# Reordering the front of a three-stage kernel: loads, order of work, constant matmuls, and the step of the sums

## The chip, the cores and the metric

The kernel runs on one core of a Trainium2 chip. The metric is device time in microseconds (us) of one execution; the median over several runs is compared. The engines are TensorE (PE, matmuls and transposes), VectorE (DVE), ScalarE (ACT), GpSimd (POOL) and SyncE (SP, which here issues nearly all DMAs).

## The reference, cut to what matters

```
# attention with 32 memory slots a head; B=4, H=8, S=576, D=64, M=32
a      = softmax(phi, over S)                     # S x M
k_m    = a.T @ k ;  v_m = a.T @ v                 # M x D each
attn   = softmax(q @ k_m.T / 8, over M)
x      = attn @ v_m                               # 2304 tokens x 512
# a gated layer, d_ff = 1536
x      = (sigmoid(x @ w_gate) * (x @ w_val)) @ w_out
# a router over 8 experts (noisy, top 2), each: relu(x @ w1[e]) @ w2[e], F = 1024
out    = sum over the two experts of weight * expert(x)
```

## The kernel before, in words

All of it is one launch. Matrix products in 16-bit floats are made of a high and a low half of each operand, so that one product takes three matmuls. The weights of the gated layer come as 64-bit words. A job is one block of 256 columns of `w_gate` or `w_val` (`wg`, `wv`, six each) or 256 rows of `w_out` (`wo`, six); each job has two half blocks of 512 KB. `rounded` (lines 371 to 381) turns a half block into floats: ScalarE converts the low words (375), VectorE does two operations on the high words (379, 380), GpSimd adds (381). After both half blocks ScalarE sums their squares (404), and `norm2` (86) makes from these a power of two as scale: a matmul with ones and some small VectorE operations.

The value memory of a batch is multiplied into the weights (`fold`, 245 to 266): `vs` is made on GpSimd (252), 32 small matmuls (259) give the folded weights of one unit `u` of 256 columns, ScalarE casts the high half (261) and VectorE makes the low half (263; for the first fold line 1102). Stage 1 (`stage1`, 476) multiplies the folded weights with the attention weights `x` of 192 tokens (line 488, 24 matmuls of 192 columns), then gates: ScalarE 490, VectorE 492, ScalarE 493, VectorE 494. Stage 2 (line 505) multiplies with `wo`. Then come tokens, router and the experts.

The attention of a batch (`attend`, 1053) is a generator: `features` (two groups of four heads: maximum 229, exponential 231), `memory` for each group (transposes of phi 189 and 194, their copies 192 and 195, the contraction with keys and values 204, its copy 206, transposes 212, copies 216 and 218), then `attention`: `scores` for the two groups' first 512 tokens and for the 64 left over (matmuls 284 and 281, maximum 288, subtraction 292, exponential 293), `normalised` (sum 299, then 303 or 305, reciprocal 306, multiplication on GpSimd 307), and `turned` (transposes 315, high half 324, low half 325). `values_scale` (237) gives the scale of the values.

The order on each engine follows priority. Attention runs ahead of the rest by 1000 in the front. `behind(d, o)` orders one instruction after another on an engine without a semaphore. `turns(g, ...)` advances generators by one step. `build` starts with `att_first_loads(0)`, whose order is SP's issue order; then three steps of attention, `FIRST` = 5 steps of weights, and attention on until the first scores. From there `half()` advances the weights by one half block and one step of attention follows, until the tokens of batch 0 are ready; the first `fold` is issued as soon as its scales exist. The VectorE steps of `scores`, `normalised` and `turned` are ordered behind the last half block (`self.shifted`). Then stage 1 runs over six units of batch 0, with weights and the attention of batch 1 between. PSUM pools: `pg` of 4 banks, `px` and `pr` of 2 each.

## Time and profile before

| | before |
|---|---|
| median of 3 runs | 849.76 us (848.55 to 851.15) |
| profiled execution | 845.65 us, span 843.8 us |
| TensorE busy | 799.6 us (95%) |
| VectorE busy | 455.0 us (54%) |
| ScalarE busy | 440.5 us (52%) |
| GpSimd busy | 233.3 us (28%) |

The span is the time from the first to the last recorded instruction of the profiled execution. Busy shares are means over stages with different limits, so what bounds a stage is read from that stage alone. A row of a timeline merges neighbouring instructions of one line; its time is that from the start of the first to the end of the last. Matmuls overlap, so the time of a run divided by its count gives their pace, and the mean duration of one does not.

### The profile page before, as it was taken

To read this page: it belongs to the slowest core of one execution; us is meant where nothing else is said; L and a number is where in the kernel's file an instruction comes from. 1 tells how busy PE (TensorE), PEld (TensorE's weight loads), DVE (VectorE), ACT (ScalarE), POOL (GpSimd) and SP (SyncE) were. 2 spreads that over 40 slices of the span, in tenths; PEclk is the share of its full clock that TensorE was granted. 3 is DMA by queue.
4 is the path that set the end of the run, shared out by engine and by line. 5 is a ranking of instruction groups with operands and counts; after the bars stand their busy time and mean duration, and the time that the engine had idled before them with its cause. 6 is when DMAs were issued, how large, how long until landed. Compare 5 with 4: busy or idle time off the path is not lost.

```text
span 843.8 us, 16766 instructions
## 1 busy us (share of the span) xinstructions
PE 799.6 (95%) x6555; PEld 528.5 (63%) x6555; DVE 455.0 (54%) x1223; ACT 440.5 (52%) x860; POOL 233.3 (28%) x258
## 2 busy tenths in 40 slices
PE   5699789999999999999999999999999999999995
PEld 3478656576677766776566565746657475574753
DVE  3788987363748698655472365543445344450210
ACT  4677786154545576534163476645556364461321
POOL 1755640012203040231135442023133231322012
PEclk9999989999999999999999999999999999999998
DMA  9987758421132656617948899536767757473103
GB/s 310 367 250 241 236 186 291 131 82 27 31 93 59 204 171 177 228 40 183 278 122 208 166 244 209 176 74 131 189 152 126 200 118 183 74 113 51 24 13 50
DMA packets 124737, 130.95 MB, mean 155 GB/s; under 512 B 71680, under 2 KB 88416, under 8 KB 124272
## 3 DMA queue, kind: packets, MB, share of 16 engines
q1 hardware_dynamic: 114480, 109.10, 45.4%
q0 software_dynamic: 10176, 20.76, 13.6%
q8 instruction: 52, 0.85, 0.4%
q14 instruction: 29, 0.24, 0.1%
HBM read 85.87 MB, written 28.76 MB: 136 GB/s over the span
## 4 chain that ended last, share of the span: by engine, by line
PE 79%; DVE 6%; ACT 6%; DMA 5%; issue 2%; SPq 1%; POOL 0%; DVEq 0%; POOLq 0%; ACTq 0%
PE py L881 24%; PE ph L857 21%; PE px L505 14%; PE pg L488 13%; PE pv L259 2%; PE pa L284 2%; PE pa L204 1%; DMA w<-wg 1%; DMA xt<-row 1%; DMA xg<-xs,mts 1%; DVE pg L492 1%; DMA w<-wo 1%; ACT wq L261 1%; DVE gT L494 1%; DMA xe<-xg 1%
## 5 line engine op out<-in xcount | busy, mean ns | idle before, releaser
L488 PE MATMUL pg<-x,wq 128*128 128x192 f16 x1728 | 162.9, 250 | 12.4 <-DVE gT L494 6.3
L881 PEld LDWEIGHTS <-hT 128*128 128x128 f16 (+1 forms) x984 | 101.9, 105 | 102.9 <-DVE hT L863 1.1
L488 PEld LDWEIGHTS <-wq 128*128 128x128 f16 x1728 | 146.3, 100 | 31.4 <-issue 17.6
L505 PE MATMUL px<-wo,gT 128*128 128x512 f16 x648 | 147.9, 379 | 0.0
L886 POOL DMA_INDIRECT out<-y,mts x39 | 63.1, 1619 | 201.9 <-ACT y L885 199.7
L881 PE MATMUL py<-w2a,hT 128*128 128x512 f16 (+1 forms) x480 | 105.3, 379 | 0.6 <-DVE hT L863 0.6
L881 PE MATMUL py<-w2b,hT 128*128 128x512 f16 (+2 forms) x504 | 104.9, 369 | 0.0
L505 PEld LDWEIGHTS <-gT 128*128 128x128 f16 x648 | 61.7, 98 | 67.7 <-issue 2.3
L857 PE MATMUL ph<-xe,w1a 128*128 128x312 f16 (+2 forms) x768 | 103.3, 296 | 0.0
L857 PE MATMUL ph<-xe,w1b 128*128 128x312 f16 (+2 forms) x768 | 103.0, 296 | 0.0
L863 DVE TENSOR_TENSOR hT<-r,hT 128x312 f16<-128x312 f32 (+2 forms) x128 | 57.4, 480 | 81.2 <-ACT hT L862 80.8
L885 ACT ACTIVATE y<-py,css 128x512 f32<-128x512 f32 (+2 forms) x41 | 27.7, 676 | 124.7 <-PE py L881 122.6
L857 PEld LDWEIGHTS <-w1b 128*128 128x128 f16 x768 | 75.0, 98 | 27.2
L857 PEld LDWEIGHTS <-w1a 128*128 128x128 f16 x768 | 74.9, 98 | 27.2
L861 ACT ACTIVATE r<-ph 128x312 f32<-128x312 f32 (+2 forms) x128 | 49.7, 428 | 73.6 <-PE ph L857 70.0
L659 POOL DMA_INDIRECT meta<-mt,vi x36 | 38.1, 1058 | 114.4 <-DVE vi L656 47.6
L842 POOL DMA_INDIRECT xg<-xs,mts x40 | 44.3, 1108 | 84.1 <-DMA xe<-xg 49.9
L490 ACT ACTIVATE sg<-pg,gss 128x384 f32<-128x384 f32 x72 | 41.7, 581 | 37.8 <-PE pg L488 37.5
L493 ACT ACTIVATE gT<-pg 128x384 f16<-128x384 f32 x72 | 35.1, 488 | 49.5 <-DVE pg L492 49.4
L492 DVE SCALAR_TENSOR_TENSOR pg<-sg,pg 128x384 f32<-128x384 f32 x72 | 40.1, 558 | 35.6 <-PE pg L488 23.0
L868 DVE TENSOR_TENSOR css<-mts,iw 128x1 f32<-128x1 f32 (+1 forms) x40 | 6.4, 162 | 88.5 <-ACT y L885 81.8
L862 ACT CAST hT<-r 128x312 f16<-128x312 f32 (+2 forms) x128 | 53.1, 458 | 0.9
(243 smaller groups left out, 954.2 us busy)
## 6 DMA issues: line engine op xcount, KB each, us to landing
wo<-w SPq DMA_DIRECT2D x52, 512.0 KB, 5.4
st<-kv SPq DMA_DIRECT2D x16, 512.0 KB, 7.3
w<-wo SPq DMA_DIRECT2D x12, 512.0 KB, 4.3
f<-w SPq DMA_DIRECT2D x12, 512.0 KB, 4.8
wsp<-hl SPq DMA_DIRECT2D x12, 512.0 KB, 3.7
out<-z SPq DMA_DIRECT2D x23, 256.0 KB, 3.3
xs<-row SPq DMA_DIRECT2D x18, 256.0 KB, 2.3
st<-q SPq DMA_DIRECT2D x6, 576.0 KB, 5.6
```

The source lines that it names most:

```text
L488: self.gated = nc.tensor.matmul(p[:, f, :], w[:, l, g, j, f * P : (f + 1) * P], x[:, r, g, ch * QC : (ch + 1) * QC], start=n == 0, stop=n ...
L490: self.tanh = nc.scalar.activation(sg, ps[0], AF.Tanh, scale=self.gs[(b, u)])
L492: nc.vector.scalar_tensor_tensor(pv, sg, 1.0, pv, op0=ALU.add, op1=ALU.mult)
L505: nc.tensor.matmul(p, g[:, l, f % 2, t * P : (t + 1) * P], self.wob[f // 2][:, r, f % 2, :], start=f + i == 0, stop=f == FT - 1 and i == 2)
L659: d = nc.gpsimd.indirect_dma_start(out=self.meta, out_offset=bass.IndirectOffsetOnAxis(ap=vi[:, t, k : k + 1], axis=0), in_=mt[:, t, k, :] ...
L842: self.nc.gpsimd.indirect_dma_start(out=xg.rearrange("p a b -> p (a b)"), out_offset=None, in_=self.xs[:rows, :], in_offset=bass.IndirectO ...
L857: self.first = nc.tensor.matmul(p[:, : t1 - t0], w1[:, l, k, f * P : (f + 1) * P], xe[:, x, t0:t1], start=n == 0, stop=n == 3 * KT - 1)
L861: nc.scalar.activation(r, p[:, : t1 - t0], AF.Relu, scale=2.0 ** -19)
L862: d = nc.scalar.copy(self.hT[:, 0, f, t0:t1], r)
L863: self.parted = d, nc.vector.tensor_sub(self.hT[:, 1, f, t0:t1], r, self.hT[:, 0, f, t0:t1])
L881: d = nc.tensor.matmul(py, self.hT[:, l, f, i * P : i * P + m], w2[:, w, f, cols], start=n == 0, stop=n == 3 * F2T - 1)
L886: d = nc.gpsimd.indirect_dma_start(out=self.out.rearrange("n (a f) -> (n a) f", a=parts), out_offset=bass.IndirectOffsetOnAxis(ap=ix[c][:m ...
```

## The change

Loads: the keys and values of both groups come first, then a half block, the queries of group 0, a half block, the queries of group 1. Order: phi of both groups is turned before either group's contraction; only two half blocks (`FIRST` = 2) are worked on ahead of the scores; the conversion of a half block on ScalarE is ordered behind the copies of phi; the identity is ordered ahead of the first maximum, and an exponential of one column is issued at the start. `fill` issues constant matmuls (all ones, 128x512, 16 bit) into a PSUM tile that is about to be overwritten, at eight places in the code. In `normalised`, the sums of batches 1 to 3 are written two words apart, and line 303's operation with two inputs becomes an addition with one input and a reciprocal into another tile.

```diff
@@ -61,7 +61,8 @@
 WAIT_KEYS, WAIT_LOADS = 2, 3
 
 AHEAD, AHEAD1 = 1000, 160
-FIRST = 5
+FIRST = 2
+FILL = {"turn": 9, "keys": (2, 4), "mean": 4, "scores": (2, 2, 0), "sv0": 6, "fold": 10, "turned": (2, 2, 1), "first": 2}
 EB = NT
 NBLK = E * EB + 1
 
@@ -89,7 +90,10 @@
         nc = self.nc
         for _ in range(before):
             yield
-        pt = self.pr.tile([P, 512], F32, tag="pr", name="pmx")[:, :n]
+        pt = self.pr.tile([P, 512], F32, tag="pr", name="pmx")
+        if tag in FILL:
+            self.fill(pt, FILL[tag])
+        pt = pt[:, :n]
         d = nc.tensor.matmul(pt, self.onef, m, start=True, stop=True)
         if tag == "wo":
             self.behind(d, self.combined)
@@ -106,6 +110,13 @@
         nc.vector.tensor_scalar(iv, h, 50 << 23, None, op0=ALU.add)
         return s.bitcast(F32), iv.bitcast(F32)
 
+    def fill(self, t, n):
+
+        for _ in range(n):
+            d = self.nc.tensor.matmul(t.rearrange("p (a b) -> p a b", a=4), self.full, self.full.unsqueeze(1).to_broadcast([P, 4, P]), start=True, stop=True)
+            if self.mark is not None:
+                self.behind(d, self.mark)
+
     def consts(self):
         nc = self.nc
         cp = self.cp = self.ctx.enter_context(self.tc.tile_pool(name="const", bufs=1, side="left"))
@@ -113,10 +124,13 @@
         jp = tmp.enter_context(self.tc.tile_pool(name="tmp", bufs=1, side="right")).tile([P, P], F32, name="jp")
         nc.gpsimd.iota(jp, pattern=[[1, P]], base=0, channel_multiplier=-1, allow_small_or_imprecise_dtypes=True)
         self.idf = cp.tile([P, P], F32, name="idf")
-        nc.vector.tensor_scalar(self.idf, jp, 0.0, None, op0=ALU.is_equal)
+        self.made = nc.vector.tensor_scalar(self.idf, jp, 0.0, None, op0=ALU.is_equal)
+        self.full = cp.tile([P, P], F16, name="full")
+        nc.vector.memset(self.full, 1.0)
         self.onef = cp.tile([P, P], F32, name="onef")
         nc.vector.memset(self.onef, 1.0)
         tmp.close()
+        nc.scalar.activation(cp.tile([P, 1], F32, name="warm"), self.onef[:, :1], AF.Exp)
         self.wss = cp.tile([P, B, UN, 2], F32, name="wss")
         self.gss = cp.tile([P, B, UN, 1], F32, name="gss")
 
@@ -166,7 +180,7 @@
         self.al[(b, what, g)] = t
 
     def att_first_loads(self, b):
-        for x in (("phi", 0), ("phi", 1), ("kv0", 0), ("kv1", 0), "w", "w", ("kv0", 1), ("kv1", 1), "w", ("q", 0), "w", ("q", 1)):
+        for x in (("phi", 0), ("phi", 1), ("kv0", 0), ("kv1", 0), ("kv0", 1), ("kv1", 1), "w", ("q", 0), "w", ("q", 1)):
             if x == "w":
                 self.wload_next()
             else:
@@ -185,19 +199,26 @@
         t = al[(b, "phi", g)]
         ag = a2.tile([P, SC + 1, P], F32, tag="a", name="a")
         pt = self.bank(b)
+        if b == 0 and g == 0:
+            self.fill(self.flat(pt), FILL["turn"])
         for c in range(SC):
             d = nc.tensor.transpose(pt[:, c, :], t[:, c * P : (c + 1) * P], self.idf)
             if b == 1:
                 self.behind(d, self.gated)
         nc.scalar.copy(ag[:, :SC, :], pt)
         pt = self.bank(b)
-        nc.tensor.transpose(pt[:SH, 0, :], t[:, SC * P :], self.idf)
-        nc.scalar.copy(ag[:SH, SC, :], pt[:SH, 0, :])
+        d = nc.tensor.transpose(pt[:SH, 0, :], t[:, SC * P :], self.idf)
+        if b == 0:
+            self.mark = d
+        self.laid = nc.scalar.copy(ag[:SH, SC, :], pt[:SH, 0, :])
         yield
         parts = [(c, P if c < SC else SH) for c in range(SC + 1)]
         kv = [al[(b, f"kv{i}", g)].rearrange("p c (h f) -> p c h f", h=2) for i in range(2)]
 
-        pm = self.flat(self.bank(b))[:, : 2 * D]
+        pm = self.flat(self.bank(b))
+        if b == 0:
+            self.fill(pm, FILL["keys"][g])
+        pm = pm[:, : 2 * D]
         for c, n in parts:
             for j in range(4):
                 rows = slice(32 * j, 32 * j + 32)
@@ -207,9 +228,14 @@
         if g == 0 and b:
             self.att_load(b, "q", 0)
         yield
-        pk = self.flat(self.bank(b))[:, : 2 * P].rearrange("p (x m) -> p x m", x=2)
+        pk = self.flat(self.bank(b))
+        if b == 0:
+            self.fill(pk, FILL["mean"])
+        pk = pk[:, : 2 * P].rearrange("p (x m) -> p x m", x=2)
         for x in range(2):
-            nc.tensor.transpose(pk[:, x, :], km[:, x].rearrange("p a d -> p (a d)"), self.idf)
+            d = nc.tensor.transpose(pk[:, x, :], km[:, x].rearrange("p a d -> p (a d)"), self.idf)
+        if b == 0:
+            self.mark = d
         kt = pk[:, 0, :].rearrange("p (a b) -> p a b", a=2)
         for j in range(2):
             rows, cols = slice(64 * j, 64 * j + 64), slice(32 * j, 32 * j + 32)
@@ -226,7 +252,7 @@
         for g in range(2):
             t = al[(b, "phi", g)]
             mx = a2.tile([P, 1], F32, tag="pmx", name="pmx")
-            nc.vector.tensor_reduce(mx, t, axis=AX.X, op=ALU.max, negate=True)
+            self.behind(nc.vector.tensor_reduce(mx, t, axis=AX.X, op=ALU.max, negate=True), self.made)
             sm = a2.tile([P, 1], F32, tag="psm", name="psm")
             nc.scalar.activation(t, t, AF.Exp, bias=mx, accum_out=sm)
             nc.vector.tensor_scalar(sm, sm, 1e-9, None, op0=ALU.add)
@@ -252,6 +278,8 @@
         nc.gpsimd.tensor_tensor(vs.rearrange("p j h m -> p j (h m)"), self.flat(vb).unsqueeze(1).to_broadcast(wide), s.unsqueeze(2).to_broadcast(wide), op=ALU.mult)
         t = self.wq[(b, u)] = self.wqp.tile([P, 2, 2, 2, 256], F16, tag="wq", name="wq")
         pv = [self.pg.tile([P, 2, 256], F32, tag="pg", name="pv") for _ in range(2)]
+        if not self.tokens_ready:
+            self.fill(self.flat(pv[0]), FILL["fold"])
         for j in range(2):
             for h in range(4):
                 for g in range(2):
@@ -274,6 +302,8 @@
 
             nt = 1 if u == 2 else SC
             ps = self.pg.tile([P, SC, P], F32, tag="pg", name="pa")
+            if b == 0:
+                self.fill(self.flat(ps), FILL["scores"][u])
             for pr in range(2):
                 cols = slice(pr * 64, pr * 64 + 64)
                 if u == 2:
@@ -295,15 +325,12 @@
 
         def normalised(ps, ex, n):
             sm = a2.tile([P, 4 * SC], F32, tag="ssm", name="ssm")[:, :n]
-            tot = sm if b else ps[:, 0, :n]
+            tot = a2.tile([P, 4 * SC, 2], F32, tag="tot", name="tot")[:, :n, 0] if b else ps[:, 0, :n]
             d = nc.vector.tensor_reduce(tot, ex, axis=AX.X, op=ALU.add)
             if b < 2:
                 self.behind(d, self.shifted)
-            if b:
-                nc.vector.scalar_tensor_tensor(sm, tot, 1e-9, tot, op0=ALU.add, op1=ALU.max)
-            else:
-                nc.vector.tensor_scalar(sm, tot, 1e-9, None, op0=ALU.add)
-            nc.vector.reciprocal(sm, sm)
+            nc.vector.tensor_scalar(tot, tot, 1e-9, None, op0=ALU.add)
+            nc.vector.reciprocal(sm, tot)
             nc.gpsimd.tensor_tensor(ex, ex, sm.unsqueeze(2).to_broadcast([P, n, M]), op=ALU.mult)
             return ex
 
@@ -311,6 +338,8 @@
             nt = 1 if u == 2 else SC
             at = ex.rearrange("p (t h) m -> p t (h m)", t=nt)
             pt = self.bank(b)
+            if b == 0:
+                self.fill(self.flat(pt), FILL["turned"][u])
             for t in range(nt):
                 self.mark = nc.tensor.transpose(pt[:, t, :], at[:, t, :], self.idf)
                 if b == 1:
@@ -373,8 +402,7 @@
         nc = self.nc
         lo, hi = t[:, :, 0], t[:, :, 1]
         d = nc.scalar.activation(lo, lo.bitcast(U32), AF.Copy, scale=2.0 ** -29)
-        if self.tokens_ready:
-            self.behind(d, o or self.copied)
+        self.behind(d, (o or self.copied) if self.tokens_ready else self.laid)
         w = self.px.tile([P, DM], F32, tag="px", name="pw").bitcast(I32)
         nc.vector.tensor_scalar(w, hi, 3, 0x3FFFFFFF, op0=ALU.logical_shift_left, op1=ALU.bitwise_and)
         self.shifted = nc.vector.scalar_tensor_tensor(v, hi, -0x40000000, w, op0=ALU.bitwise_and, op1=ALU.bitwise_or)
@@ -481,7 +509,10 @@
         if (blk, u) not in self.gT:
             self.gT[(blk, u)] = self.gp.tile([P, 2, 2, BLK], F16, tag="gT", name="gT")
         o, w, x = self.gT[(blk, u)], self.wq[(b, u)], self.xT[b]
-        ps = [self.pg.tile([P, 512], F32, tag="pg", name="pg")[:, : 2 * QC].rearrange("p (f s) -> p f s", f=2) for _ in range(2)]
+        ps = [self.pg.tile([P, 512], F32, tag="pg", name="pg") for _ in range(2)]
+        if not self.firsts[0]:
+            self.fill(ps[0], FILL["first"])
+        ps = [p[:, : 2 * QC].rearrange("p (f s) -> p f s", f=2) for p in ps]
         for j, p in enumerate(ps):
             for f in range(2):
                 for n, (g, l, r) in enumerate(((0, 0, 0), (0, 0, 1), (1, 0, 0), (1, 0, 1), (0, 1, 0), (1, 1, 0))):
@@ -1057,8 +1088,12 @@
             while b > 1 and self.firsts[b - 2] < UN * S // QC:
                 yield
             self.xT[b] = self.xp.tile([P, 2, 2, S], F16, tag="x", name="x")
-            yield from self.memory(b, 0)
-            yield from self.memory(b, 1)
+            ms = [self.memory(b, g) for g in range(2)]
+            if b == 0:
+                for m in ms:
+                    yield next(m)
+            for m in ms:
+                yield from m
             att = self.attention(b)
             if b == 0:
                 for _ in range(2):
@@ -1083,7 +1118,7 @@
         self.folded, self.firsts = [0] * B, [0] * B
         atts, weights = attentions(), self.weights()
         offset[atts] = AHEAD
-        turns(atts, atts, atts)
+        turns(atts, atts, atts, atts)
         turns(*[weights] * FIRST)
         while not self.less:
             turns(atts)

```

## Rows read from the trace of the kernel before

**Rows 1.** Table of stretches: us, busy time of each engine (instructions), PEclk, DMA share.

```profile
0.00:42.80 42.80, 24.59 (x186) 18.27 (x186) 24.90 (x65) 23.97 (x51) 19.49 (x29) 1.00 0.98 339
42.80:90.00 47.20, 44.45 (x573) 37.37 (x574) 41.95 (x93) 35.63 (x79) 25.05 (x31) 1.00 0.74 230
90.00:115.00 25.00, 16.68 (x203) 13.70 (x200) 23.98 (x47) 19.64 (x38) 17.43 (x21) 0.93 0.62 195
115.00:131.00 16.00, 15.48 (x179) 10.37 (x180) 14.25 (x41) 13.99 (x28) 4.38 (x23) 0.79 0.91 286
```

**Rows 2.** Timeline of PE, 148 to 172 us: start, us, engine, line, operation.

```profile
...
150.33 18.73 PE L505 MATMUL px<-wo,gT 128*128 128x512 f16 x86
...
```

**Rows 3.** Timeline of PE in the front; in brackets idle before and releaser.

```profile
7.35 1.09 PE L189 MATMUL pa<-idf,phi 128*128 128x128 f32 x4 [7.35 <-DVE new L957]
...
19.62 5.22 PE L284 MATMUL pa<-kbd,gT 128*128 128x64 f32 x24
...
32.91 2.42 PE L259 MATMUL pv<-w,vs 64*32 64x256 f32 x32 [4.20 <-POOL vs L252]
...
42.79 5.61 PE L488 MATMUL pg<-x,wq 128*128 128x192 f16 x44 [0.40 <-DVE wq L1102]
```

**Rows 4.** Timeline of PE, 80 to 93 us.

```profile
81.50 2.00 PE L284 MATMUL pa<-kbd,st 128*128 128x64 f32 x16
...
88.10 4.68 PE L488 MATMUL pg<-x,wq 128*128 128x192 f16 x54
```

**Rows 5.** Timeline of DVE in the front.

```profile
12.29 0.70 DVE L379 TENSOR_SCALAR pw<-w 128x512 int32<-128x512 int32 x1
...
17.45 0.69 DVE L379 TENSOR_SCALAR pw<-w 128x512 int32<-128x512 int32 x1 [3.75 <-DMA w<-wv]
...
20.30 0.69 DVE L379 TENSOR_SCALAR pw<-w 128x512 int32<-128x512 int32 x1 [1.44 <-DMA w<-wv]
...
27.40 0.69 DVE L288 TENSOR_REDUCE smx<-pa 128x16 f32<-128x512 f32 x1 [1.49 <-PE pa L284]
...
40.86 0.68 DVE L325 SCALAR_TENSOR_TENSOR x<-pa,x 128x512 f16<-128x512 f32 x1
```

**Rows 6.** DMA issues to 30 us: count, KB each, median us to landing.

```profile
st<-kv SPq DMA_DIRECT2D x4, 512.0 KB, 7.5
w<-wg SPq DMA_DIRECT2D x4, 512.0 KB, 6.8
...
gT<-q SPq DMA_DIRECT2D x4, 288.0 KB, 8.1
phi<-phi SPq DMA_DIRECT2D x2, 288.0 KB, 3.0
st<-kv SPq DMA_DIRECT2D x4, 64.0 KB, 6.2
```

**Rows 7.** Groups by line and shape, DVE to 42.8 us: busy us, mean ns.

```profile
L380 DVE SCALAR_TENSOR_TENSOR w<-w,pw 128x512 int32<-128x512 int32 x6 | 4.1, 683 | 0.1
L380 DVE SCALAR_TENSOR_TENSOR w<-wo,pw 128x512 int32<-128x512 int32 x6 | 4.1, 682 | 0.0
```

**Rows 8.** Timeline of DVE: line 306 in the front, line 303 in batch 1.

```profile
33.77 0.25 DVE L306 RECIPROCAL ssm<-ssm 128x16 f32<-128x16 f32 x1
...
93.25 0.82 DVE L303 SCALAR_TENSOR_TENSOR ssm<-ssm 128x16 f32<-128x16 f32 x1
...
98.21 1.19 DVE L303 SCALAR_TENSOR_TENSOR ssm<-ssm 128x4 f32<-128x4 f32 x1
```

**Rows 9.** All instructions of line 303: count, duration ns min/median/max, first and last start.

```profile
L303 DVE SCALAR_TENSOR_TENSOR ssm<-ssm x9: 100/164/1193, 85.3 to 262.5; 128x16 f32<-128x16 f32 x6, 128x4 f32<-128x4 f32 x3
```

**Rows 10.** Timeline of GpSimd (POOL) beside the rows of 8.

```profile
32.81 2.55 POOL L381 TENSOR_TENSOR w<-w,wo 128x512 int32<-128x512 int32 x2
...
91.49 2.54 POOL L381 TENSOR_TENSOR wo<-wo,w 128x512 int32<-128x512 int32 x2
...
96.84 2.54 POOL L381 TENSOR_TENSOR wo<-wo,w 128x512 int32<-128x512 int32 x2 [0.45 <-DVE pg L492]
```


## The prediction

> **What bounds the kernel now.** I read first the table of stretches, to see where TensorE (PE) is not busy [rows 1]. In the front, up to 42.80 us, PE is busy 24.59 us and idle 18.2; from 42.80 to 90 it is idle 2.75; from 90 to 115 it is idle 8.3 of 25 while VectorE (DVE) is busy 23.98; from 115 to 131 PE is nearly always busy, but the granted clock is 0.79. Behind that the work is PE's own: 86 matmuls of stage 2 run without a gap in 18.73 us, 0.216 each [rows 2]. So time can be won only ahead of 131 us, and there are two ledgers: PE's, which decides until about 90, and DVE's, which decides from 90 to about 131, since DVE makes the rounded weights, the gates and their low halves.
>
> Next the timeline of PE in the front [rows 3]. The reader is to see three things. PE's first matmul starts at 7.35 us. The 24 score matmuls take 5.22 us, 0.218 each, where 16 of the same form take 2.00 us later, 0.125 each [rows 4]. The first long run of stage 1 takes 5.61 us for 44, 0.128 each, where 54 take 4.68 us later, 0.087 each. The PEclk column says 1.00 over the front [rows 1], but the pace of like instructions says that PE runs there at the lower of its two levels, 1.2 instead of 2.4 GHz, with idle gaps before and between its work; and since 0.128 lies between 0.087 and twice that, the level rises only inside that first run. I go by the pace.
>
> Then DVE's timeline [rows 5]. It waits 3.75 us (to 17.45) and 1.44 us (to 20.30) for the third and fourth half block, and 1.49 us for the second group's scores (to 27.40). From 27.40 on it hardly stops until the second token block's low half at 40.86. Between these two rows it works through six half blocks among the steps of attention, because the order is written out: one half block, one step. So the start of stage 1 (the run at 42.79 waits for DVE) is set by when the second score maximum can start.
>
> **The change, part by part.**
>
> *Loads.* The sizes are in [rows 6]: phi 288 KB a group, keys and values 576 KB a tile (512 + 64), a half block 512, queries 576 a group. In the old order the second half block is complete at 2752 KB (phi, keys of group 0, two half blocks) and DVE got it at 12.29; the fourth is complete at 5504 KB and DVE got it at 20.30. That is 2752 KB in 8.0 us, 344 KB a us. In the new order: keys of group 1 complete at 2880 KB, 12.7 us; first half block 3392 KB, 14.2; queries 0 3968 KB, 15.8; second half block 4480 KB, 17.3; queries 1 5056 KB, 19.0; third half block 5568 KB, 20.5; fourth 6080 KB, 22.0. SP issues in this order and nothing is added to its queue; each later load is only as late as the bytes put ahead of it. So keys come earlier and the fourth half block 1.7 us later than before.
>
> *Front order.* Exp's table is loaded ahead of phi, and the identity is pinned ahead of the first maximum, so PE can turn phi somewhat before 7.35. This is worth nothing by itself: the keys of group 1, 12.7 us, cover it. Without that cover it would be worth a microsecond or two of PE, still ahead of DVE's wait for half block 2.
>
> *DVE in the new front.* Half block 2 lands at 17.3, takes 0.69 + 0.68 [rows 5, 7] and ends at 18.7. The first maximum and subtraction (0.69 and much the same, about 1.4) are tied behind it: 20.1. The third half block lands at 20.5 and ends at 21.9. The scores of group 1 need queries 1 (19.0) and 16 matmuls, 2.0 at full clock, 3.5 at the lower: 21.0 or 22.5. So the second maximum starts at 21.9 instead of 27.40, 5.5 us earlier. From there the order holds the same six half blocks before the same token block, so the same 13.46 us, and stage 1's run starts near 37.3. The fold should be no obstacle: before, it began 12.6 us after DVE took the fourth half block (20.30 to 32.91, with PE's long score run between); DVE now takes that block at 23.3, so the fold begins by 35.9 at the latest, likely some us earlier.
>
> *What is then undone.* Nine half blocks are rounded at that point instead of eleven. Two remain for later: 2 x 1.37 = 2.7 us of DVE. Their lower bound is this own time; the upper bound is the pace of the stretch that receives them: 12 of the 36 half blocks were done by 42.8 [rows 7], so 24 take the 88.2 us to 131, 3.7 each, 7.4 for two. I take 2.7, since ScalarE and GpSimd, which share each half block, have room there [rows 1].
>
> *Fill.* 50 constant matmuls of 512 columns are added (9 + 6 + 8 + 4 + 6 + 10 + 5 + 2, each place by its count in `FILL`). At the pace of stage 2 they cost 10.8 us of PE, at half of it 21.6. Their cover is PE's idle time: 7.35 us before the first matmul, 4.20 before the fold [rows 3], and what the raised clock sets free. PE's old front work is 24.6 at the lower level; by the two score rows (0.218 and 0.125) it is 14.1 at the higher. 14.1 + 10.8 = 24.9 fits into 37.3. So the fills cost nothing if the clock rises. What they give: 44 stage-1 matmuls at 0.087 instead of 0.128, 1.8 us for PE.
>
> *Sums two words apart.* In batch 1, line 303 (two inputs in SBUF) took 0.82 and 1.19 us, where nine of them have a median of 0.16 and a least of 0.10 [rows 8, 9]; both long ones end with GpSimd's line 381 beside them, at 94.0 and 99.4 [rows 10]. That is 1.75 us of DVE in the stretch that DVE bounds. Bounds of the saving: 0 if the new add waits too, 1.75 if not. No row shows an add with such a step. The nearest is the reciprocal at 33.77, one input in SBUF, which took its 0.25 while GpSimd ran line 381 from 32.81 [rows 8, 10]. I take 1.75. The other seven, at the median, have nothing to give.
>
> The Trainium skill speaks against this part: "VectorE: DVE Perf Modes", section "What auto-detection actually checks", lets a one-source operation from SBUF to SBUF use both ports when its outermost sizes are even or equal, and names no step; "SBUF — State Buffer", section "Who interferes with whom", says that such an operation and GpSimd exclude each other. By these pages the new add would wait as line 303 does, and the sum would be 3.3 instead of 5.0. No run here shows it yet.
>
> *Sum.* DVE's ledger: 5.5 - 2.7 + 1.75 = 4.5. PE's ledger is ahead by 5.5 + 1.8 = 7.3, of which DVE can use only what it now loses waiting: it is idle 5.25 us between 42.80 and 90 [rows 1], mostly on short chains; bounds 0 and 1.8, I take 0.5 because DVE, at 96% from 90 on, ends the part. Gain 5.0. The profiled execution took 845.65 (span 843.8), so 840.7 in its terms; the median of the three runs shown is 849.76, 4.1 above it, so I forecast 844.8.
>
> **The rivals.**
>
> *The add still waits* (sum without 1.75): 846.5. For it: both long rows end exactly when GpSimd does, so the port is real. Against it: the reciprocal row. 0.18.
>
> *Two half blocks at the stretch's pace* (7.4 instead of 2.7): 5.5 - 7.4 + 1.75 = about 0, 849.8. For it: PE idles 8.3 us between 90 and 115 beside DVE's 96%, so the stretch is chained, not only loaded; and the last weights now come later behind the same token work. Against: DVE is 96% busy there, so its work decides. 0.19.
>
> *PE keeps its whole lead:* 7.3 + 1.75 = 9.0, 840.7. It needs DVE's idle time before 90 to vanish. 0.11.
>
> *The fills don't raise the clock* (the other side). Then PE's front is 24.6 + 21.6 = 46.2, all in PE's order, and stage 1 starts near 46 instead of 42.79. It decides from the point where PE's front exceeds 42.8: with 24.9 at the higher level and 46.2 at the lower, that is when over 84% of it runs at the lower. Stage 1 starts 3.5 late, of which the saved DVE time returns a little: 852.5. For it: the lower level lasted 45 us in the old front. Against: that front had gaps of 7.35 and 4.20 us, which the fills close, and the level did rise in the first dense run. 0.09.
>
> **How the numbers follow.** Forecast 0.43, the others as given. A change under 0.3% (2.5 us) can't be told from none here. Faster: 0.43 + 0.11 + 0.15 of the first rival = 0.69. Within: 0.03 + 0.17 of the second = 0.20. Slower: 0.09 + 0.02 = 0.11. The range runs from the whole lead (840.3, with the 1 us by which runs differ) to the second rival (850.5) and leaves out the last; the forecast's own range, from the bounds of the clock and of the loads, is 842 to 847.2.
>
> **What would show it.** Right: fills from about 1 us, score matmuls at 0.125 each, second maximum near 22, stage 1's run from 36 to 39 at 0.087 each, nine or ten half blocks rounded by then, the new add at about 0.16 beside GpSimd, and DVE again over 90% until its weights end, 4 to 6 us earlier than 131. Wrong: a second maximum later than 24.5 (loads don't land by their bytes), an add of 0.8 or 1.2 us, a PE row that ends a wait for fills, or PE idle of more than 11 us between 90 and 131, which would show the lead given back.

## The result and the profile after

The changed kernel is slower: 855.72 us median (852.75 to 858.60) against 849.76 (846.71 to 854.84), a ratio of 1.0076 with an interval of 1.0057 to 1.0094. Forecast were 844.8 and a range to 850.5. The profiled execution took 852.75 us, the fastest of the nine; its span is 850.9.

The table of stretches of the kernel after, against [rows 1]:

```profile
0.00:42.80 42.80, 30.15 (x238) 17.62 (x239) 22.17 (x59) 22.14 (x48) 16.02 (x24) 0.88 0.93 314
42.80:90.00 47.20, 41.11 (x565) 33.90 (x563) 41.51 (x94) 36.36 (x79) 25.41 (x30) 1.00 0.75 242
90.00:115.00 25.00, 16.98 (x236) 13.96 (x240) 23.03 (x50) 18.57 (x37) 17.29 (x20) 0.96 0.68 217
115.00:131.00 16.00, 14.86 (x197) 10.47 (x182) 13.54 (x38) 13.78 (x29) 7.01 (x28) 0.86 0.63 186
```

VectorE is less busy in every stretch: 22.17 instead of 24.90, 41.51 instead of 41.95, 23.03 instead of 23.98, 13.54 instead of 14.25. TensorE is busy 3.34 us less between 42.80 and 90, but with 565 instructions instead of 573; part of this is pace, since 44 matmuls at 0.097 us in place of 0.128 are 1.4 us less of busy time.

TensorE's timeline in the front, against [rows 3] (line 116 is the fill, 236 the turning of the key means, 314 the scores, 344 the turned steps, 519 stage 1):

```profile
10.45 1.04 PE L116 MATMUL pa<-full 128*128 128x512 f16 x4
15.78 0.69 PE L236 MATMUL pa<-idf,km 128*128 128x128 f32 x2 [4.29 <-ACT km L227]
16.26 1.91 PE L116 MATMUL pa<-full 128*128 128x512 f16 x4
18.10 2.52 PE L225 MATMUL pa<-st,a 128*32 128x128 f32 x40
...
24.26 1.90 PE L314 MATMUL pa<-kbd,gT 128*128 128x64 f32 x16
...
36.85 1.01 PE L116 MATMUL pa<-full 128*128 128x512 f16 x2
37.68 0.62 PE L344 MATMUL pa<-idf,ex 128*128 128x128 f32 x4
...
42.20 4.66 PE L519 MATMUL pg<-x,wq 128*128 128x192 f16 x48
```

and VectorE's, against [rows 5]:

```profile
14.66 0.69 DVE L407 TENSOR_SCALAR pw<-w 128x512 int32<-128x512 int32 x1 [8.20 <-DMA w<-wg]
...
17.51 0.69 DVE L407 TENSOR_SCALAR pw<-w 128x512 int32<-128x512 int32 x1 [1.44 <-DMA w<-wg]
...
24.03 0.69 DVE L318 TENSOR_REDUCE smx<-pa 128x16 f32<-128x512 f32 x1 [5.10 <-PE pa L314]
...
26.43 0.68 DVE L318 TENSOR_REDUCE smx<-pa 128x16 f32<-128x512 f32 x1
```

The first two half blocks landed by their bytes (14.66 and 17.51; forecast 14.2 and 17.3), the scores ran at 0.12 each, stage 1's first 48 matmuls at 0.097. But the key means waited, the second maximum came at 26.43 and not 21.9, and the run at 42.20 and not 37.3. (In the kernel before, the first four of these 48 matmuls start at 41.60 and the other 44 at 42.79.) ScalarE's timeline says why:

```profile
14.66 0.71 ACT L404 ACTIVATE w<-w 128x512 int32<-128x512 uint32 x1 [6.54 <-DMA w<-wg]
15.22 0.51 ACT L227 ACTIVATE km<-pa,psm 128x256 f32<-128x256 f32 x1
```

The conversion of the first half block stands ahead of the key means in ScalarE's order and waits for its load; the means' matmuls had ended near 10.5. Behind the means, four fills (16.26, 1.91 us) stand ahead of the second group's contraction (18.10), which then starts without a wait.

Behind the front, TensorE shows two waits that the kernel before doesn't have in this size (its timeline, 86 to 99 us):

```profile
86.64 1.49 PE L519 MATMUL pg<-x,wq 128*128 128x192 f16 x16 [2.08 <-DVE ex L322]
...
97.34 1.10 PE L287 MATMUL pv<-w,vs 64*32 64x256 f32 x32 [3.49 <-POOL vs L278]
```

The second is a fold, waiting for GpSimd's scaled values:

```profile
94.22 1.28 POOL L409 TENSOR_TENSOR wo<-wo,w 128x512 int32<-128x512 int32 x1
95.60 0.27 POOL L480 TENSOR_SCALAR wss<-sws,sv0s 128x2 f32<-128x2 f32 x1
...
96.67 0.61 POOL L278 TENSOR_TENSOR vs<-vb,wss 128x256 f32<-128x256 f32 x1
```

They need the norm of their unit's weights (line 109, made at 94.21). In the second profile of the kernel before, the same step of GpSimd (`vs` of the sixth unit) is 6.3 us earlier, and no fold waits for it between 47 and 150 us:

```profile
89.12 0.27 POOL L452 TENSOR_SCALAR wss<-sws,sv0s 128x2 f32<-128x2 f32 x1
...
90.38 1.18 POOL L252 TENSOR_TENSOR vs<-vb,wss 128x256 f32<-128x256 f32 x2
```

The new add, against [rows 9], is short here; the longest of its nine takes 0.245 us (durations in ns):

```profile
L332 DVE TENSOR_SCALAR tot<-tot x9: 105/165/245, 86.5 to 263.3; 128x16 f32<-128x16 f32 x6, 128x4 f32<-128x4 f32 x3
```

### The profile page after: what moved, and what is told of

Same layout as the page of the kernel before. It is cut to its first block, busy times and chain, and to the rows that moved or that the text cites. A ratio compares the mean times of both kernels' runs of the same rounds, so it can differ in the third digit from the quotient of the medians.

```text
span 850.9 us, 16864 instructions
## 1 busy us (share of the span) xinstructions
PE 803.3 (94%) x6605; PEld 524.9 (62%) x6605; DVE 452.7 (53%) x1224; ACT 441.5 (52%) x861; POOL 231.6 (27%) x258
## 5 line engine op out<-in xcount | busy, mean ns | idle before, releaser
L519 PEld LDWEIGHTS <-wq 128*128 128x128 f16 x1728 | 144.0, 99 | 27.7 <-issue 12.8
```

What stands on the lines that cost most here:

```text
L519: self.gated = nc.tensor.matmul(p[:, f, :], w[:, l, g, j, f * P : (f + 1) * P], x[:, r, g, ch * QC : (ch + 1) * QC], start=n == 0, stop=n ...
```

## The experiments

The table has all kernels with their medians and ratios to the kernel before. Behind these stand three figures from the one profile of each: VectorE's busy time from 0 to 112 us (table of stretches), the start of the sum over the wo norms, which ends the weights' chain, and the start of stage 2's first matmul. "Blocks" is the number of half blocks ahead of the first score maximum.

| kernel | blocks, fills | us | ratio | VectorE | norms | stage 2 |
|---|---|---|---|---|---|---|
| before, second profile | 4, 0 | 848.77 | 0.9994 (0.9975 to 1.0012) | 88.06 | 115.6 | 122.2 |
| const_only | 4, 0 | 848.74 | 0.9992 (0.9980 to 1.0005) | 88.77 | 114.7 | 121.1 |
| sums_only | 4, 0 | 850.19 | 1.0006 (0.9989 to 1.0024) | 90.59 | 112.1 | 117.4 |
| fill_only | 4, 50 | 848.21 | 0.9991 (0.9975 to 1.0007) | 89.51 | 114.2 | 118.8 |
| first5 | 4, 0 | 847.58 | 0.9975 (0.9959 to 0.9991) | 89.11 | 114.0 | 118.6 |
| first5_idle_fill | 4, 37 | 849.60 | 1.0015 (0.9999 to 1.0031) | 89.55 | 113.4 | 118.0 |
| thin_fill | 4, 43 thin | 850.50 | 1.0014 (0.9998 to 1.0029) | 88.23 | 115.2 | 120.6 |
| first5_fill | 4, 50 | 851.64 | 1.0023 (1.0009 to 1.0036) | 88.53 | 115.1 | 121.7 |
| first5_km_off | 4, 43 | 852.19 | 1.0027 (1.0016 to 1.0038) | 88.61 | 114.6 | 121.1 |
| two_back | 2, 0 | 849.99 | 1.0009 (0.9994 to 1.0024) | 88.76 | 115.0 | 120.3 |
| two_back_fill | 2, 50 | 850.73 | 1.0026 (1.0011 to 1.0042) | 87.60 | 115.4 | 120.7 |
| two_late | 2, 0 | 851.93 | 1.0024 (1.0003 to 1.0045) | 85.26 | 118.0 | 122.6 |
| no_fill | 2, 0 | 852.49 | 1.0032 (1.0017 to 1.0048) | 86.81 | 121.0 | 129.6 |
| no_fill_again | 2, 0 | 851.59 | 1.0025 (1.0001 to 1.0048) | 83.78 | 123.8 | 132.4 |
| first4 | 3, 0 | 855.17 | 1.0071 (1.0057 to 1.0085) | 83.89 | 120.1 | 127.6 |
| km_first | 2, 50 | 853.83 | 1.0045 (1.0029 to 1.0061) | 83.00 | 125.1 | 133.7 |
| km_off | 2, 43 | 855.55 | 1.0071 (1.0049 to 1.0094) | 84.87 | 122.4 | 131.0 |
| changed kernel | 2, 50 | 855.72 | 1.0076 (1.0057 to 1.0094) | 83.72 | 123.6 | 132.2 |
| changed, second profile | 2, 50 | 854.44 | 1.0052 (1.0024 to 1.0081) | 82.07 | 126.1 | 134.8 |

**km_first** puts ScalarE's key means of both groups ahead of the conversion, to test ScalarE's order.

```
-        self.laid = nc.scalar.copy(ag[:SH, SC, :], pt[:SH, 0, :])
+        nc.scalar.copy(ag[:SH, SC, :], pt[:SH, 0, :])
-        nc.scalar.activation(km, ...)
+        self.laid = nc.scalar.activation(km, ...)
-        turns(atts, atts, atts, atts)
+        turns(*[atts] * 7)
```

> The changed kernel with one thing moved: ScalarE converts the first half block of weights behind the key means of both groups, not ahead of the first. Theory A (ScalarE's order in front of the key means undid the early loads): means at about 11 and 15.5 us instead of 15.22 and 20.76, the maxima at about 18 and 21.5 us instead of 24.03 and 26.43, stage 1's run at 38 to 39 us instead of 42.20, and the time 3 to 4 us under the changed kernel's 855.7, so about 852. Rival B (the stage's middle is bound by the weights, which end later because only two half blocks stand in front): the front moves as in A, but the two are level again by 165 us and the time stays at 855 to 857. Rival C (something else holds the key means): the maxima stay past 23 us.

The means came at 11.11 and 15.08, the maxima at 19.17 and 23.27, the run at 39.67: that the conversion held the front is shown. The time, 853.83, lies between theory A's and rival B's, and its interval overlaps the changed kernel's. The norms came at 125.1 (123.6 and 126.1 in the changed kernel's two profiles), so what the front gained wasn't there when the weights ended: rival B's reason, though not its time.

**no_fill**: all counts of `FILL` set to 0; **no_fill_again** is the same kernel.

> The changed kernel without its 50 constant matmuls; the constant tile and everything else stay. Theory A (the fills raise the granted clock early and do nothing else): the clock is at its lower level until stage 1 has run for some time, as before (first rise at 46.3 us), the run's 48 first matmuls take about 6.1 us instead of 4.66, the time is 1 to 2 us above the changed kernel's, 857. Rival B (the 50 more matmuls at the head of TensorE's program are what makes the part behind 165 us lose 7 us in steps): that part takes as long as in the kernel before, and the time is about 850. Rival C (the fills cost nothing and gain nothing): 855 to 856.

It is faster than the changed kernel (intervals apart), so none of the three was right. The front did what the prediction had said. ScalarE's means (12.13) are ahead of the conversion (14.85) again, with `self.laid` as in the changed kernel. This is so in all six profiles of the new order without fills, and in none of the three with fills and ScalarE's order left alone (the changed kernel's two, first5_fill): the fills brought the hold about. no_fill's VectorE, then its TensorE:

```profile
19.30 0.69 DVE L318 TENSOR_REDUCE smx<-pa 128x16 f32<-128x512 f32 x1 [0.18 <-PE pa L314]
...
21.96 0.68 DVE L318 TENSOR_REDUCE smx<-pa 128x16 f32<-128x512 f32 x1
```

```profile
17.59 2.57 PE L314 MATMUL pa<-kbd,gT 128*128 128x64 f32 x22
...
37.39 2.88 PE L519 MATMUL pg<-x,wq 128*128 128x192 f16 x17
```

> The changed kernel without fills, for a second profile. Theory A (with two half blocks fewer in front, what is lost is lost ahead of 250 us, where stage 2 waits for the weights): at 250 us it stands 2 to 5 us behind the kernel with FIRST = 5. Rival B (it is level at 250 us and loses later): within 1 us of it there, and 4 us behind at the end.

Here the second maximum came at 24.10 and the run at 39.28. TensorE, then VectorE:

```profile
16.75 4.79 PE L314 MATMUL pa<-kbd,gT 128*128 128x64 f32 x22
...
39.28 5.89 PE L519 MATMUL pg<-x,wq 128*128 128x192 f16 x48
```

```profile
24.10 0.69 DVE L318 TENSOR_REDUCE smx<-pa 128x16 f32<-128x512 f32 x1 [1.49 <-PE pa L314]
```

To say where time is lost, like instructions are compared: the one that VectorE starts at 250 us in the first profile of the kernel before, and the same one, counted from the end, in the others. There no_fill_again is 3.2 us behind first5, and from there on both lose the same (4.3 and 4.4 against the first profile of before): theory A. no_fill's own profile doesn't show this loss: it is 0.1 us behind first5's at 250 us, and level with it at the end (848.20 and 848.14). It is the fastest of its eight executions. The kernel is the same, and its 22 score matmuls took 2.57 us there and 4.79 here.

**sums_only**: the kernel before with the sums two words apart and the plain add alone.

> The kernel before with the sums two words apart alone. Theory A (the long adds of 0.82 and 1.19 us go, up to 1.75 us of VectorE in the stage, and the rest is as before): the adds of batches 1 and 2 take under 0.3 us each, the time is 848.0 to 849.8. Rival B (the wider tile shifts what is allocated or queued later, and the part behind 165 us loses 7 us): 856.

The time is as before, and neither theory holds: an add of 1.2 us stays. VectorE, then GpSimd:

```profile
90.80 0.55 DVE L302 TENSOR_SCALAR tot<-tot 128x16 f32<-128x16 f32 x1
...
95.48 1.21 DVE L302 TENSOR_SCALAR tot<-tot 128x4 f32<-128x4 f32 x1
```

```profile
90.02 1.29 POOL L378 TENSOR_TENSOR wo<-wo,w 128x512 int32<-128x512 int32 x1 [0.56 <-ACT sg L487]
...
94.11 2.54 POOL L378 TENSOR_TENSOR wo<-wo,w 128x512 int32<-128x512 int32 x2 [0.45 <-ACT w L372]
```

Both adds end within 0.05 us of GpSimd's instruction beside them (91.35 and 91.31, 96.69 and 96.65), as line 303 did in [rows 8] and [rows 10]. So the step of two words frees nothing; in the changed kernel the adds only met GpSimd less. By the Trainium skill ("VectorE: DVE Perf Modes", "What auto-detection actually checks", and "SBUF — State Buffer", "Who interferes with whom") this add would exclude GpSimd as line 303 did, and the trace agrees.

**const_only**: the kernel before with the constant tile and the early exponential.

> The kernel before with the constant tile of 256 bytes a partition, its memset and the one early exponential, without any fill; all tiles allocated behind it lie at other addresses. Theory A (addresses don't matter): 849.8, within 0.3%. Rival B (the shifted addresses make the part behind 165 us lose 7 us in steps): about 857, with the steps of 0.6 to 1.4 us where the changed kernel has them.

Theory A. The steps in which this profile too loses time behind 165 us are in the last section.

**first5**: `FIRST = 5` and no fills; **first4**: `FIRST = 4` and no fills; **first5_fill**: the changed kernel with `FIRST = 5` alone.

> The changed kernel without fills, with all four half blocks in front of the first maximum as before (only the order of the loads, both groups' keys ahead of the weights, and the sums differ from the kernel before). Theory A (the loads by bytes make the half blocks land 5 us later, and the maxima stand behind them): half block 4 is done at 24 to 25 us and the first maximum behind it, the second at 25 to 27, the run starts at 41 to 42, the time is 849 to 851. Rival B (keys first is a gain by itself): the run starts before 40 us and the time is 847.

> The changed kernel without fills and with three half blocks in front of the first maximum (FIRST = 4), between the two of 852.5 us and the four of 847.6. Theory A (each half block taken from the front is paid behind it): the wo norms are summed at 116 to 119 us, and the time is 849 to 851. Rival B (only the number of gates ahead of the sum of the norms counts, 18 here, 17 and 19 at the ends; the front's gain is worth as much as the delay): the time is at one of the ends.

> The changed kernel with one number undone: four half blocks of weights in front of the first maximum again, not two (FIRST = 5). Theory A (the two half blocks are most of the loss): the wo norms are summed at 113 to 115 us instead of 123.6, stage 2 starts at 119 to 121 instead of 132.2, and the time is 848 to 850, some 6 to 7 us under the changed kernel's 855.7. Rival B (the fills and ScalarE's order cost 3 us whatever stands in front): 851 to 852.

With four half blocks and no fills the time is 847.58, the best here and under the kernel before by more than the measurement's interval. The front is theory A's (second maximum 26.40, first matmul of stage 1 at 41.32), the time nearer rival B's. With the fills it is 851.64, rival B's. So undoing `FIRST` gives 4.1 us with fills and 4.9 without, the intervals apart both times. first4, with three half blocks, is not between its neighbours: it is as slow as the changed kernel, and neither theory had that. Its VectorE worked 34.91 us between 47 and 90, first5's 39.63: it lost mostly in the stage.

**two_back** and **two_back_fill** (the latter on km_first): two more half blocks behind the first maximum.

```
+        more = iter(range(2))
         while not self.tokens_ready:
             half()
+            if next(more, None) is not None: half()
             turns(atts)
```

> The changed kernel without the fills, with two half blocks of weights more in the loop behind the first score maximum, so that from the second maximum on VectorE's order is that of the kernel before (13 half blocks ahead of the first gate of stage 1, the sum of the wo norms behind gate 17 and not 19). Theory A (the early front is real, and is given back because two half blocks fewer stand in front of every later step, so that the weights end late and stage 2's first matmul waits for them: 129.6 us without the fills, 121 to 122 in the kernel before): the second maximum is at about 23 us, stage 1's run starts at 38 to 40, the wo norms are summed at 110 to 112 instead of 121.0, stage 2 starts at 117 to 119, and the time is 847, 5 us under the changed kernel without fills (852.5). Rival B (the two half blocks are not what makes the weights end late): the sum of the norms stays at 119 or later and the time at 852. Rival C (the two half blocks take the front's gain back in full): the run starts at 41 to 42 and the time is 850.

> The same two half blocks put back, with the fills and with ScalarE's conversion of the first half block behind the key means of both groups. Theory A (the fills cost only by what they did to ScalarE's order): 847 to 848, as the one without fills. Rival B (the fills cost of themselves, by standing ahead of real matmuls in TensorE's order or by the clock falling more often later): 850 to 851, and the granted clock falls at least as often between 80 and 125 us as without them.

The weights were back in time (norms at 115.0, stage 2 at 120.3) and the time came down to 849.99, but the second maximum was at 23.29 and the run at 41.41: rival C. The two half blocks cost in the front what they save behind. With fills it is 850.73, in rival B's range, but only 0.7 above two_back, and the intervals overlap: a cost of the fills isn't shown in this order.

**two_late**: no_fill with `half()` twice between the front and the first fold of stage 1's loop.

> The changed kernel without fills, with two half blocks of weights more between the front and stage 1's first fold (13 half blocks done at the first gate or shortly behind it, the norms' sum behind gate 17). Theory A (the front's gain is kept and the folds no longer wait for the weights' norms): the second maximum at 22 to 24 us, stage 1's run at 38 to 40, no wait of TensorE over 1 us for GpSimd's scaled values (3.36 to 3.49 us at 96 to 98 us with two half blocks fewer), stage 2's first matmul at 116 to 119, the time 845 to 847. Rival B (VectorE's work up to the end of the weights is what counts, and an early front only moves idle time): stage 2 starts at 118 to 121 as with FIRST = 5, and the time is 847 to 850.

No fold waits for GpSimd any more, but between 47 and 150 us TensorE's stage 1 waits 2.5 us for VectorE's folded weights and 1.6 for the scores' step (0.4 and 0.5 in first5), and the norms are at 118.0. The time, 851.93, is worse than both theories. So taking away the fold's wait doesn't bring the time back; that VectorE's lateness stands behind both (B's reason) fits these rows and is not shown by them.

**fill_only**: the kernel before with the 50 fills; **km_off**: km_first without the seven fills ahead of the turned steps and stage 1; **first5_km_off**: km_off with `FIRST = 5`; **first5_idle_fill**: that without the six ahead of the value norm; **thin_fill**: first5_km_off with each fill cut to one column.

> The kernel before with the 50 constant matmuls at the same places, the constant tile and the early exponential, nothing else. Theory A (fills raise the clock and cost nothing): the clock is full from about 7 us, stage 1's first 48 matmuls take 4.5 to 5 us instead of 6.7 to 6.8, the run ends 2 us earlier, and the time is 848 to 849. Rival B (fills cost by themselves, 3 us as between the changed kernel and the one without them): 852 to 853, and it shows either as matmuls of the front that start later behind fills or as more time at the lower clock between 80 and 125 us.

> The changed kernel with the key means ahead of ScalarE's conversion and without the seven fills ahead of the turned steps and of stage 1's first matmul. Theory A (those seven stand on the path: two of them, 0.9 to 1.0 us, ahead of each group's transposes whose input is there): stage 1's run starts 2 us earlier than with them (39.67), at 37.5 to 38 us, and the time is 852 to 853 against 853.8. Rival B (they only fill idle time): the run starts at 39.5.

> The changed kernel with FIRST = 5, the key means ahead of ScalarE's conversion, and only the fills that stand ahead of work not yet ready (those ahead of the turned steps and of stage 1 are out). Theory A (the clock's gain of 1.4 us, as of the fills alone on the kernel before, adds to the 847.6 of the same order without fills): the run's first 48 matmuls take 4.6 us, and the time is 846 to 847. Rival B (VectorE's order holds the stage and the clock's gain is lost in waits): 847.6 within 1 us.

> The changed kernel with FIRST = 5, the key means ahead of ScalarE's conversion, and fills only where TensorE waits for loads or for the first fold (no six ahead of the matmul of the value norm, none ahead of the turned steps and stage 1). Theory A (a fill costs only where it stands ahead of work whose input is there; the six took 2.72 us ahead of the norm's matmul, and VectorE waited 1.91 us for it): VectorE doesn't wait there, stage 1's run starts at 41.3 us as without fills, and the time is 846.5 to 848. Rival B (the fills cost as such, through the clock or through TensorE's longer program): 851 to 852.

> The kernel with FIRST = 5, the key means first and 43 fills (852.2), each fill cut to one column: as many instructions, nearly no work. Theory A (what fills cost is their time on TensorE: ahead of ready work in the front, and by the clock later): 847 to 849, as the same order without fills (847.6), and from 250 us to the end it takes what kernels without fills take. Rival B (43 more matmuls and weight loads in TensorE's program cost as such): 851 to 852.5.

fill_only: stage 1's run ended at 46.94 (const_only 47.60, before_again 48.58); the time is theory A's, and its interval holds no change. km_off: the run started at 37.71 as theory A has it, 2.0 earlier than km_first's, yet the time was not better. first5_km_off: worse than both expectations; its TensorE and VectorE show six fills, at the lower clock, ahead of a matmul that VectorE needs:

```profile
26.22 2.72 PE L116 MATMUL pmx<-full 128*128 128x512 f16 x6
28.74 0.43 PE L97 MATMUL pmx<-vm,onef 128*128 128x1 f32 x2
```

```profile
29.20 0.23 DVE L105 TENSOR_SCALAR pmx<-pmx 128x1 int32<-128x1 int32 x2 [1.91 <-PE pmx L97]
```

Without those six (first5_idle_fill) the wait is gone and the median is 2.6 us lower, 849.60 (the intervals overlap), between its two theories. It is still 2.0 above first5, and there the intervals don't overlap; but the two differ by the key means' place in ScalarE's order as well as by the fills. thin_fill, 850.50, lies between its two theories.

**after_again** and **before_again**: both kernels, for a second profile.

> The changed kernel, for a second profile. Theory A: 3 to 6 us behind the kernel before at 250 us, and no more than 1 to 2 us lost from there on. Rival B: level at 250 us as in its first profile, with 5 us lost behind it.

> The kernel before, for a second profile, to compare with: both theories expect 848 to 851 us, with the stalls of 0.6 to 1.2 us between 310 and 332 us that every profile but the first of it shows.

At 250 us the changed kernel stood 3.8 us behind the one before (first profiles: 1.0), and 3.0 at the end (first profiles: 7.1, of which 2.9 are the stalls of the last section). The second pair is theory A, the first pair nearer rival B: where the loss falls differs from execution to execution.

## Why the prediction was wrong

**VectorE's work.** The table of stretches of the second profiles of the kernel before and the changed one, then of first5:

```profile
0.00:15.00 15.00, 5.67 (x52) 3.95 (x52) 5.32 (x17) 6.27 (x14) 3.55 (x11) 1.00 0.89 284
15.00:47.00 32.00, 23.28 (x161) 18.38 (x162) 22.74 (x54) 19.39 (x41) 18.39 (x20) 1.00 0.99 356
47.00:90.00 43.00, 40.39 (x547) 33.51 (x546) 38.79 (x87) 33.89 (x76) 22.60 (x29) 1.00 0.72 226
90.00:112.00 22.00, 15.54 (x191) 12.74 (x188) 21.22 (x41) 16.85 (x33) 14.47 (x17) 0.92 0.68 222
```

```profile
0.00:15.00 15.00, 8.32 (x65) 3.76 (x65) 3.13 (x15) 4.89 (x11) 0.97 (x9) 0.98 0.90 279
15.00:47.00 32.00, 25.05 (x214) 16.57 (x214) 22.00 (x54) 19.36 (x42) 18.21 (x20) 0.85 0.92 323
47.00:90.00 43.00, 37.06 (x520) 30.31 (x519) 38.23 (x85) 34.27 (x75) 22.20 (x26) 1.00 0.75 240
90.00:112.00 22.00, 17.09 (x202) 14.22 (x200) 18.71 (x42) 14.94 (x30) 13.58 (x17) 0.84 0.62 186
```

```profile
0.00:15.00 15.00, 8.15 (x81) 5.42 (x84) 3.15 (x15) 5.39 (x12) 0.97 (x9) 1.00 0.88 280
15.00:47.00 32.00, 18.49 (x140) 13.70 (x134) 25.07 (x58) 20.54 (x44) 21.07 (x22) 0.63 1.01 364
47.00:90.00 43.00, 40.84 (x560) 33.97 (x558) 39.63 (x89) 35.25 (x78) 23.89 (x33) 1.00 0.72 229
90.00:112.00 22.00, 15.05 (x182) 12.44 (x180) 21.26 (x42) 17.36 (x35) 14.63 (x15) 0.92 0.62 207
```

The third figure with a count is VectorE's. Both new orders do 2.2 us less in the first 15 us, for want of a half block. first5 makes it good by 47 (25.07 against 22.74). The changed kernel loses 0.7 more to 47, 0.6 to 90 and 2.5 to 112, and is 6.0 us of work behind; its median lost 6.0. Over the 19 rows of the table and the first profile of before, the medians go with VectorE's work done by 112 us (correlation -0.81). But this is a split into two groups: twelve profiles above 87 us, with medians of 847.58 to 852.19, and eight below, with 851.59 to 855.72. Within the groups the correlation is -0.24 and -0.36, and sums_only, with the most work (90.59), has a median of 850.19. So the figure tells the kernels that fell behind in the stage from the others; it doesn't price the loss and doesn't show its cause.

**Point by point.**

*Loads*: right.

*Front order*: right in no_fill's profile (second maximum 21.96, run at 37.39), 2 us late in no_fill_again's, where the scores ran at the slower pace (24.10, 39.28), and wrong with the fills (26.43, 42.20). The step looked at VectorE's order and the loads, and not at ScalarE's, where with the fills the conversion came ahead of the key means.

*What is then undone* is the step that failed: it turned the sign even without the fills. The two half blocks were priced at 2.7 us, their own time, with 7.4 as the other bound. Undoing `FIRST` alone gives 4.9 us without fills and 4.1 with them, although the front starts stage 1 later then. Profile by profile, no_fill starts stage 1 3.9 us ahead of first5 and ends level; no_fill_again starts 2.0 ahead and ends 3.2 behind. So 4.0 and 5.3 us were given back (up to 6.5, counted from the end of the first 48 matmuls). The rival at 7.4 was right that own time is too little, and too high in size. Without the sums it would give 851.7, near no_fill's 852.49 and 851.59; since the front gained less than its 5.5 in the second profile, this nearness is partly luck.

Why own time is too little is argued, not shown. Each fold needs its unit's norm, and later steps stand behind the folds. From 90 to 112 us VectorE is busy 18.71 us instead of 21.22; from 90 to 125 us it waits 1.9 us for stage 1's matmuls and 1.2 for loads in the changed kernel's second profile (nothing and 0.6 in the second of before). But two_late took the folds' wait away and won nothing, and first4 says that it isn't a price per half block. The cause of the size stays open.

*Sums*: 1.75 predicted, nothing found (sums_only); the rival that the add still waits was right.

*Fills*: the clock did rise (the run at 0.097 each), but "cost nothing" was wrong. They cost 3.2 us in the changed kernel (no_fill; 2.9 in the second measurement of both, where the intervals overlap) and 4.1 with `FIRST = 5`. In the changed kernel a part may be the hold that they brought about: km_first, without it, is 1.9 lower, with an interval that overlaps both the changed kernel's and no_fill's. Seen in the front are four ahead of the second group's contraction (1.91 us), six ahead of the value norm (VectorE waits 1.91 us in first5_km_off) and those ahead of turned steps and stage 1 (the run 2.0 earlier without, km_off); that these make the time was not shown. That the cover is idle time was right for TensorE in sum and wrong by place.

*Sum*: in place of 5.0 us won, the order without fills loses 2.7 (no_fill) and the fills 3.2 more.

**Open.** Behind 250 us, eight of the nine profiles with fills of full width lose 4.5 to 10.5 us against the first profile of before (fill_only 3.1), and nine without fills 3.1 to 5.3. Three of the former (km_first, the changed kernel's second, km_off) have the lower clock for 3.4 us there, from 443.6, 444.5 and 720.5, each within 1 us behind a wait of TensorE of 1.98, 1.85 and 3.07 us; none of the latter has, though before_again waits 2.4 us there too. So it is open why the 50 fills cost nothing on the kernel before and 4.1 us with `FIRST = 5`; whether the 2.0 us of first5_idle_fill are the fills' or those of the key means' place; and thin_fill didn't tell the fills' work from their number. Why first4 is slower than both its neighbours was not tried further; VectorE's work says only where.

## What to carry to other kernels

An earlier first result is worth nothing if work that was done in its place is only put off: compare how far the engine that bounds a stage has come by the stage's end. The own time of work that is put off is only a lower bound of its price; look for what waits for it (here a norm, a scale, a fold), and for its place in the order of every engine that it passes, not only of the one that bounds. Filler work ahead of a ready instruction delays it by its full time, and it can change the order on other engines. When a change has several parts, undo each alone, with and without the others, as with `FIRST` and the fills here; and go by medians, since two profiles of one kernel can tell opposite stories.

## What was not expected of the hardware

**Stalls that one profile lacks.** The profile on which the prediction was built lacks stalls that all others here show, whatever the kernel: between 308 and 330 us they lose 2.2 to 3.3 us against it, at like instructions. ScalarE, first and second profile of the same kernel:

```profile
308.39 1.07 ACT L261 CAST wq<-pv 128x512 f16<-128x512 f32 x2 [0.21 <-PE pv L259]
```

```profile
311.60 1.07 ACT L261 CAST wq<-pv 128x512 f16<-128x512 f32 x2 [2.34 <-PE pmx L93]
```

The fold whose result it casts was done by 309.4 in the second. The cause stays open. Part of a difference between two single profiles (7.1 us between the first ones of the two kernels) belongs to no change.

**The clock of the front.** Which of its two levels TensorE has in the front is not decided by the edits alone. Ahead of its scores sums_only has no edit against the kernel before; yet 16 of its score matmuls ran at 0.12 us each, the pace of [rows 4], where those of [rows 3] ran at 0.218:

```profile
18.61 1.90 PE L284 MATMUL pa<-kbd,gT 128*128 128x64 f32 x16
...
38.84 0.80 PE L485 MATMUL pg<-x,wq 128*128 128x192 f16 x4 [1.06 <-DVE x L322]
```

Its stage 1 starts at 38.84 instead of 41.60, without any of the change's front. The same holds between no_fill (0.117 a score matmul) and no_fill_again (0.218). What decides it wasn't tried. It is a rival to each reading here that compares the fronts, or VectorE's work, of single profiles; the medians are taken over 6 to 12 executions of each kernel.
